# Order of the first loads, place of two groups of bulk loads, and a last stage that multiplies out of PSUM, in a kernel that mixes a long convolution with local attention

## The chip, the cores and the metric

The kernel runs on one core of a Trainium2 chip. The metric is the device time of one execution in microseconds. Before the change three runs took 224.1, 224.79 and 225.97 us; the median is 224.79. One execution of the same program was profiled; all rows below are of it, with times counted from its first instruction.

TensorE (PE in the rows; PEld is its weight load) multiplies matrices into PSUM, VectorE (DVE) and ScalarE (ACT) work element by element and empty PSUM, GpSimd (POOL) fills and copies in SBUF and issues DMAs, SyncE (SP) issues DMAs only. Each executes its own instructions in the order in which they are written and waits on semaphores where it needs another's result.

## The reference

Two branches over the same 2048 x 640 inputs are mixed by a gate (all bf16, batch of one):

```python
# A: causal long convolution of k_shift * v along the sequence, times q
k_shift = sum(k_pad[:, t:t + S] * shift_k[:, ks - 1 - t] for t in range(4))
kv = k_shift * v
y = causal_conv(kv, ssm_k) + kv * ssm_D          # in the reference by FFT of length 4096
a = q * y
# B: 32 heads of 20, each query sees 8 keys at distances 0, 2, ..., 14
qkv = x @ wqkv                                   # x is the same tensor as A's q
o = softmax(q . k_window / sqrt(20)) . v_window
b = o @ wo
# mix
g = sigmoid((x * gate_w).sum(-1))
out = g * a + (1 - g) * b
```

## The kernel before

The work is a set of generators ("streams"), each of which yields requests: `P` for TensorE, `A` or `D` or `AD` for ScalarE or VectorE, `G` for GpSimd, `S` for SyncE. `Steps.run` reads the string `ORDER` (L115): each letter names a stream and grants its next request, a `-` in front picks the second of two allowed engines. So `ORDER` fixes the instruction order of every engine by hand; the costs in the requests only document it. A stream that takes PSUM gets one of four double banks of the tile `PS`, first in, first out, and gives it back with the eviction.

The streams of the change, by their letter: `a` xpose, `c` fragger with the bulk loads inside it, `d` score_gen, `f` conv, `g` conv_v, `i` qkproj, `j` gate, `l` h_slot, `s` outproj, `t` final, `u` and `v` load_q(0) and load_q(1), `w` and `x` vproj(0) and vproj(1), `y` and `z` the forward transforms of the filter h.

The stages, in order of time:

- **Start** (`heads`, L396, and `xpose`, L439). x is loaded in eight pieces of 256 rows (`xn`, L413) on SP's queue, with the first half of the value weights (`Wv`, L407) after piece 0 and the first query and key weights (`Wqk`, L411) after piece 2. While the first loads run TensorE multiplies zeros (`WARM` = 7 matmuls of 512 columns, L401), and after the transposes of piece 0 four more of 512 columns with no use for the result (L447). `xpose` turns each piece by ten transposes into PSUM (L445) and one copy of 1280 columns into `xT` (even rows of x in its first half, odd ones in its second).
- **Projections and attention.** `vproj(0)` and `vproj(1)` make the values of 16 heads each, in 18 units of five matmuls (nine blocks, even and odd rows; L521), cast into `VW` (L524). Beside each head's 20 values `VW` holds a column of ones for the sum of the softmax; three memsets write it (L431 and L433). `qkproj` makes queries and keys in five tiles of 128 columns (`ft`, L568), cast to a staging tile `stg`; `fragger` copies each head's rows from there by DMA into `qb` and `kb` (L618, on GpSimd's queue but for the first tile), where `score_gen` reads them (L642), ScalarE takes exponentials (L650) and `pv_gen` multiplies with the values (L674).
- **Bulk loads** (`bulk`, L363) come behind the copies of a tile in `fragger`: k, small tables and the first half of h behind tile 0; G (the stage matrix of the second transform step, four loads of 384 KB) and the first half of v (four loads of 320 KB) in turn behind tile 1; the second half of v behind tile 2; the second half of h behind tile 3. `paced` (L326) has GpSimd write one element of the target first, and the load on SP waits for it, so that no load starts before GpSimd has come past the copies ahead of it.
- **Convolution.** `conv` makes the shifted k (L467 to L482), `conv_v` multiplies v by it (L486), two instructions on each half of v. The transforms (L701, L705, L724), products (L756) and `inverse1` (L835) follow; `h_slot` adds the direct term to h (L773) when a half of it has landed.
- **Last stage.** `inverse1(1)` ends with casts into `UC`. `outproj` makes b in 32 units of five matmuls (16 rows t, two halves n; L869), each evicted with the factor 1 - g into `bl` (L874 on ScalarE, L876 on VectorE). `load_q` loads q and multiplies it by g (L890). `final` (L893) works on six groups of rows t, `TAIL` = (0,3), (3,3), (6,2), (8,3), (11,3), (14,2): 32 small matmuls a row into two double banks (L912); two casts into `yb`, one by each engine (L919); on VectorE `q *= yb` (L924) and `q += bl` (L926); four output DMAs (L929). The g_nat loads of the gate (L543) stand on SP's queue ahead of the second half of h.

Of the kernel before, what the change touches and what calls it, by code (L numbers as in the profile page):

```python
# [18 lines left out]
D = 640  # L19
# [28 lines left out]
WARM = 7  # L48
KROWS = [(42, 64), (20, 42), (0, 20)]
TAIL = [(0, 3), (3, 3), (6, 2), (8, 3), (11, 3), (14, 2)]  # L50
# [65 lines left out]
a-aa-aw-wa-aw-ww-wiiai-iiaaiaa-aia-iii-aiaa-ii-iiii-ii-iiiicifffccccw-wwww-wwwwfwwwwf-wffffwwwwwwcwcccccwwwdw-wdwddddi-wfccccccii  # L116
-iiidfifddiiiieiifiiffiieidddiiiiiicddiwdxwexxxxxxxxxxccccffcfffffffffeccc-xcfcccccccccccccccccccccccccccccccccccccccccccidi-iiddd
ii-iddifd-iifxdddxedidffdfddefcicccii-iddiedd-icddlie-iiiyf-yddccdixiyyfy-xe-ydddexixdxddyyfyy-xcccxcccxffcccccccccccccciiiiciiccd
ciieddffdcccffdd-iiieiifiidididxdiffffffexididxdfeidid-i-xfxxyyy-yyexyey-xyyfyxccccccccciccccc-xcccc-idddidx-i-xxddddi-x-ijdddfjff
ejiddcciddcceiiiidddiiiiiffgg-ideieddd-ii-igigddiddeddjddeyjjyyyeeyyy-yyyy-yyyycc-yyyy-ycccccyyccccccccccccccclccccdddddz-zzd-zddd  # L120
z-zzzz-zzccczz-zzzzzz-zeddddedcdzdd-zedddoezdddd-zzo-zz-zjuddedddzedzz-zzzeezzz-zzooozz-z101-0010-1u111-111111-1o101-00o00-000000o
-00001011-1r-rr-r000u0r-r10111r00o00oooo2222-r0r-r000000000oqssss11110sssssss0s01111ssss2ss21111ssss222222222oooooooo222222244111p
313333p31333333333333413333uu4uuu444444444444444u54vv55u-5555-55-55-55-5555555tuut-ttssssssvvtvvstttstssssssv-tttvtttstssvv-ssvtvs
ttstst-ttssssssstttst-ttsssssssstttts-tssstt
# [91 lines left out]
def kernel(  # L216
# [146 lines left out]
    def bulk(ft):  # L363
        if ft == 0:
            yield from load_k(1)
            yield from load_k(2)
            yield from load_corners()
            yield from small()
            yield from load_h(0)
        if ft == 1:  # L370
            for a in range(4):
                yield from load_G(a)
                yield from load_v(0, a)
        if ft == 2:
# [21 lines left out]
    def heads():  # L396
# [8 lines left out]
        for a in range(8):  # L405
            if a == 1:
# [24 lines left out]
        nc.vector.memset(VW[:, :, :, DH], 1.0)  # L431
        for j in (0, NBP):
            nc.vector.memset(VW[0:PRE, j, :, DH], 0.0)  # L433
# [5 lines left out]
    def xpose():  # L439
        for a in range(8):  # L440
# [5 lines left out]
            for n in range(0 if a else 4):  # L446
                nc.tensor.matmul(PS[:, 3, 0], lhsT=ident[:], rhs=xn[:, 0, n % 2, 0:512], start=True, stop=True, skip_group_check=True)  # L447
# [411 lines left out]
    def outproj():  # L859
# [4 lines left out]
        for t in range(16):  # L864
            for n in range(2):
                g = yield Req("P", 0.0, [ev(f"oT{ft}") for ft in range(NDT)], take=1, half=1, pe=(5, 137.0, 272.0, 133.0))
                op = psum(g)[:, 0:320]
                for ft in range(NDT):
                    nc.tensor.matmul(op, lhsT=oT[:, ft].rearrange("p h m a -> p a (h m)")[:, t, :], rhs=wo[:, ft, 320 * n:320 * n + 320],  # L869
                                     start=(ft == 0), stop=(ft == NDT - 1), skip_group_check=True)  # L870
                r = yield Req("AD", dict(A=370.0, D=400.0), [g.done], give=g.banks)
# [5 lines left out]
            mark(f"bl{t}", r)  # L877
# [92 lines left out]
```

## Time and profile before

| | us |
|---|---|
| runs: lowest, median, highest | 224.1, 224.79, 225.97 |
| profiled execution, first to last instruction (its span) | 222.5 |
| of it busy: TensorE matmuls, VectorE, ScalarE, GpSimd | 204.3, 185.0, 174.9, 51.1 |
| first matmul on a piece of x | 4.57 |
| first query unit | 10.33 |
| last matmul of the second inverse step begins | 194.85 |
| first matmul of the last stage | 196.22 |
| last instruction of VectorE begins | 217.46 |

The profile gives no other time of the profiled execution than its span; the runs lie 1.6 to 3.5 us above that. A timeline row reads: start, length, engine, line, operation, output and inputs, count, and in brackets how long the engine had stood idle before and what ended that. Rows with a count are several instructions merged into one. SPq, ACTq and POOLq are the engines' own queues of issues.

### The profile page before, as it was taken

What the parts mean: (1) busy time and instruction counts of PE and PEld (TensorE: products, weight loads), DVE (VectorE), ACT (ScalarE), POOL (GpSimd) and SP (SyncE); (2) the same over time, 40 slices, a digit from 0 to 9 for tenths busy, and PEclk for the clock granted to TensorE, in tenths of its full rate; (3) what the DMA queues carried; (4) which work ended last, traced back from release to release, by engine and by line L of the source; (5) the groups of instructions that cost most, each with busy time, mean ns of one, the idle gap of its engine ahead of it and who ended that gap; (6) DMA issues with size and microseconds to landing.
All of it is one profiled execution on the core that took longest, in us unless ns stands there. A gap on an engine that the chain in (4) does not pass through costs nothing.

```text
span 222.5 us, 8401 instructions
## 1 busy us (share of the span) xinstructions
PE 204.3 (92%) x3577; PEld 165.8 (75%) x3577; DVE 185.0 (83%) x261; ACT 174.9 (79%) x253; POOL 51.1 (23%) x129
## 2 busy tenths in 40 slices
PE   7999999999999999699997867999999999979990
PEld 3777987696777577466685756889888899979880
DVE  4745778997998898569898978998999997859992
ACT  0264487769998898599999988998999999478770
POOL 7980711470617044402450000000000000000000
PEclk9999999999999999999999699999999999999999
DMA  6999789599999999803993396678567082003645
GB/s 199 349 237 275 188 180 205 133 168 149 208 182 197 163 151 155 140 4 52 183 171 74 85 214 152 172 174 213 122 142 227 4 184 55 3 3 91 152 106 136
DMA packets 69049, 33.35 MB, mean 150 GB/s; under 512 B 51476, under 2 KB 66708, under 8 KB 69012
## 3 DMA queue, kind: packets, MB, share of 16 engines
q1 hardware_dynamic: 65684, 27.66, 61.3%
q0 software_dynamic: 2880, 4.90, 9.9%
q8 instruction: 28, 0.46, 1.0%
q10 hardware_dynamic: 448, 0.26, 0.4%
q14 instruction: 9, 0.07, 0.1%
HBM read 19.51 MB, written 2.62 MB: 100 GB/s over the span
## 4 chain that ended last, share of the span: by engine, by line
PE 51%; DVE 20%; ACT 10%; DMA 8%; issue 7%; POOL 2%; DVEq 0%; POOLq 0%; ACTq 0%
PE PS L568 14%; PE PS L521 8%; ACT ETall L650 6%; PE PS L835 6%; DMA kb<-stg 6%; DVE UC L245 5%; PE PS L869 4%; PE PS L724 4%; PE PS L674 3%; DVE SX L245 3%; PE PS L642 3%; DVE q L926 2%; DVE yb L245 2%; ACT H L243 2%; DVE q L924 2%
## 5 line engine op out<-in xcount | busy, mean ns | idle before, releaser
L650 ACT ACTIVATE ETall<-PS 121x912 bf16<-121x912 f32 (+1 forms) x80 | 63.8, 864 | 8.1 <-PE PS L642 7.7
L568 PE MATMUL PS<-xT,Wqk 128*128 128x342 bf16 (+1 forms) x300 | 49.7, 310 | 0.6 <-ACT stg L243 0.3
L243 ACT CAST UC<-PS 128x1024 bf16<-128x1024 f32 (+2 forms) x49 | 44.4, 1030 | 4.0 <-DVE UC L245 3.1
L568 PEld LDWEIGHTS <-Wqk 128*128 128x128 bf16 x300 | 27.4, 97 | 14.3 <-issue 0.5
L521 PE MATMUL PS<-WvT,xT 128*121 128x320 bf16 x180 | 27.5, 300 | 0.1
L467 DVE TENSOR_TENSOR KX<-KX 128x1280 bf16<-128x1280 bf16 x32 | 25.3, 820 | 0.3
L618 POOL DMA_DIRECT2D qb<-stg x29 | 14.6, 506 | 45.8 <-ACT stg L243 30.5
L869 PE MATMUL PS<-wo,oT 128*128 128x320 bf16 x160 | 24.4, 302 | 0.1
L521 PEld LDWEIGHTS <-xT 128*121 128x121 bf16 x180 | 23.4, 134 | 1.4
L243 ACT CAST stg<-PS 128x363 bf16<-128x363 f32 (+1 forms) x39 | 17.1, 471 | 7.8 <-PE PS L568 7.5
L869 PEld LDWEIGHTS <-oT 128*128 128x128 bf16 x160 | 21.1, 145 | 1.5 <-issue 0.5
L724 PEld LDWEIGHTS <-G 64*128 64x128 bf16 x512 | 18.2, 93 | 4.9 <-issue 3.7
L618 POOL DMA_DIRECT2D kb<-stg x36 | 18.1, 511 | 15.8 <-ACT stg L243 7.6
L642 PE MATMUL PS<-qb,kb 31*128 31x114 bf16 x576 | 16.0, 212 | 5.1 <-DMA kb<-stg 2.3
L245 DVE CAST stg<-PS 128x342 bf16<-128x342 f32 (+1 forms) x21 | 11.0, 522 | 11.7 <-PE PS L568 9.4
L642 PEld LDWEIGHTS <-kb 31*128 31x128 bf16 x576 | 9.4, 93 | 13.5 <-issue 9.8
L674 PEld LDWEIGHTS <-ETall 121*128 121x128 bf16 x576 | 17.4, 96 | 2.1 <-issue 0.5
L674 PE MATMUL PS<-VW,ETall 121*128 121x63 bf16 (+2 forms) x576 | 18.2, 184 | 0.6 <-DVE SX L245 0.3
L835 PE MATMUL PS<-F,Hw 128*128 128x128 bf16 x160 | 18.1, 219 | 0.0
L874 ACT ACTIVATE bl<-PS,omg 128x320 bf16<-128x320 f32 x31 | 16.1, 566 | 2.4 <-PE PS L869 1.9
L835 PEld LDWEIGHTS <-Hw 128*128 128x128 bf16 x160 | 17.9, 114 | 0.0
L245 DVE CAST UC<-PS 128x1024 bf16<-128x1024 f32 x13 | 15.3, 1219 | 2.6 <-ACT UC L243 1.2
(75 smaller groups left out, 334.1 us busy)
## 6 DMA issues: line engine op xcount, KB each, us to landing
xn<-in_A_q_dram SPq DMA_DIRECT2D x8, 320.0 KB
h_lin<-in_A_ssm_k_dram SPq DMA_DIRECT2D x16, 160.0 KB
vin<-in_A_v_dram SPq DMA_DIRECT2D x8, 320.0 KB
Hw<-H SPq DMA_DIRECT2D x8, 320.0 KB
q<-in_A_q_dram SPq DMA_DIRECT2D x8, 320.0 KB
Hw<-SX SPq DMA_DIRECT2D x8, 320.0 KB
kb<-stg POOLq DMA_DIRECT2D x28, 85.1 KB, 5.5
out_dram<-q SPq DMA_DIRECT2D x16, 120.0 KB
```

The source lines that it names most:

```text
L243: nc.scalar.copy(dst, src)
L245: nc.vector.tensor_copy(dst, src)
L467: eng.tensor_tensor(d, kin[:, n + 3 - j:n + 3 - j + m, :], w.to_broadcast([128, m, QC]), ALU.mult)
L521: nc.tensor.matmul(ps[0:BK, 0:320], lhsT=xT[:, dt, s0:s0 + BK], rhs=Wv[:, dt, 320 * hp:320 * hp + 320], start=(dt == 0), stop=(dt == NDT - 1))
L568: nc.tensor.matmul(ps[:, 0:n], lhsT=Wqk[:, dt, w, 128 * ft:128 * ft + 128], rhs=xT[:, dt, s0:s0 + n], start=(dt == 0), stop=(dt == NDT - 1))
L618: (nc.sync if near else nc.gpsimd).dma_start(dst[r0:r0 + rows, 0:wd], stg[fa - f0:fb - f0, 0:wd])
L642: nc.tensor.matmul(psum(g, h4 // 2)[:, h4 % 2, BQ * bb:BQ * bb + BQ], lhsT=kb[r:r + DH + NF, BK * b:BK * b + 128], rhs=qb[r:r + DH + NF, B ...
L650: nc.scalar.activation(ETall[0:BK, e, :, 0:BQ * nb], psum(g, k)[0:BK, :, 0:BQ * nb], ACT.Exp, scale=SCALE)
L674: nc.tensor.matmul(O[:, (b - b0) // 6, c0:c0 + 21 * nh], lhsT=ETall[0:BK, e, hh, BQ * bb:BQ * bb + 128], rhs=VW[0:BK, b, 4 * t + h4:4 * t ...
L724: nc.tensor.matmul(ps[:, c, 160 * jj:160 * jj + 160], lhsT=G[rows, j0 + jj, 64 - 64 * rr:192 - 64 * rr], rhs=Am[rows, rr].rearrange("p o ( ...
L835: nc.tensor.matmul(d, lhsT=st[(key, P)][:, c, o + il // 4, :, il % 4], rhs=M[:, k, :], start=(k == 0), stop=(k == 1), skip_group_check=True)
L869: nc.tensor.matmul(op, lhsT=oT[:, ft].rearrange("p h m a -> p a (h m)")[:, t, :], rhs=wo[:, ft, 320 * n:320 * n + 320], start=(ft == 0), s ...
```

## The change

At the start: piece 1 of x is loaded second and the first half of the value weights third; `WARM` is 5; the four matmuls behind piece 0's transposes are gone; piece 0 is copied in two halves (even rows, odd rows), both on VectorE; the memsets of VW's ones stand behind the copy of piece 7. In the order the two value units of block 0 come ahead of piece 2's transposes; before, one came ahead of it and one behind:

```
before:  a -a a -a w -w a -a w -w w -w i i ...
after:   a -a -a a -a w -w w -w a -a w -w i i ...
```

The bulk loads: behind tile 1 only G; behind tile 2 the first half of v; behind tile 3 the second half of v and then the second half of h, as before. Everything else in the order of the middle stays.

The last stage. ScalarE casts the first half of a group into `yb` (now half as wide), VectorE multiplies the second half straight out of PSUM, then the first half from `yb`, and adds `bl` to both. Row 15 is left out of that addition: its two projection units come last, and VectorE adds them out of PSUM with the factor 1 - g in one instruction (`scalar_tensor_tensor`), followed by the outputs of that row. The order from the last cast of the inverse step on (O8.0 is row 8, half 0 of the projection, T0 to T5 the groups; each O is the matmuls and the eviction):

```
before:  q0 scale x2, T0 matmuls, cast, cast, O5.1 O6.0 O6.1, T0 mul, q1 scale x2, O7.0, T0 add,
         T1 ..., q1 scale x6 spread over T1 and T2, ... T5 matmuls, cast, O15.0, cast, O15.1, T5 mul, T5 add
after:   O5.1 O6.0, q0 scale x2, q1 scale x8,
         T0 (matmuls, cast, PSUM mul, mul, add), O6.1 O7.0 O7.1 O8.0,
         T1, O8.1 O9.0 O9.1, T2, O10.0 O10.1 O11.0, T3, O11.1 O12.0 O12.1,
         T4 matmuls, cast, PSUM mul, mul, O13.0 O13.1, T4 add,
         T5 matmuls, cast, PSUM mul, mul, O14.0 O14.1, T5 add (row 14), O15.0 O15.1
```

Two projection units thus stand ahead of T0, the ten scalings of q stand ahead of T0's arithmetic, and of the 31 evictions that ScalarE made of the projection and the one that VectorE made, 30 are now ScalarE's and two are the fused ones.

```diff
-WARM = 7
+WARM = 5
+LATE = 15
@@ bulk
             for a in range(4):
                 yield from load_G(a)
-                yield from load_v(0, a)
         if ft == 2:
             for a in range(4):
+                yield from load_v(0, a)
+        if ft == 3:
+            for a in range(4):
                 yield from load_v(1, a)
-        if ft == 3:
             yield from load_h(1)
@@ heads
-            if a == 1:
+            if a == 2:
                 nc.sync.dma_start(Wv[:, :, 0:320], W3[:, :, 2, 0:320])
...
-        nc.vector.memset(VW[:, :, :, DH], 1.0)
-        for j in (0, NBP):
-            nc.vector.memset(VW[0:PRE, j, :, DH], 0.0)
@@ xpose
-            for n in range(0 if a else 4):
-                nc.tensor.matmul(PS[:, 3, 0], lhsT=ident[:], rhs=xn[:, 0, n % 2, 0:512], start=True, stop=True, skip_group_check=True)
-            r = yield Req("AD", dict(A=1120.0, D=735.0), [g.done], give=g.banks)
...
+            for e in ((0, 1), (1, 2)) if a == 0 else ((0, 2),):
+                last = e[1] == 2
+                r = yield Req("AD", dict(A=1120.0, D=735.0) if a else dict(A=580.0, D=450.0), [g.done], give=g.banks if last else [])
...
             mark(f"xT{a}", r)
+            if a == 7:
+                nc.vector.memset(VW[:, :, :, DH], 1.0)
+                for j in (0, NBP):
+                    nc.vector.memset(VW[0:PRE, j, :, DH], 0.0)
@@ outproj
+                if t >= LATE:
+                    yield Req("D", 400.0, [g.done, ev(f"z{t}")], give=g.banks)
+                    reg = st["q1"][:, t % 8, 320 * n:320 * n + 320]
+                    nc.vector.scalar_tensor_tensor(reg, op, omg[:, t:t + 1], reg, ALU.mult, ALU.add)
+                    if n:
+                        for gg in range(4):
+                            (nc.scalar if gg > 1 else nc.sync).dma_start(...)
+                    continue
@@ final
-        yb2 = p0.tile([128, 2, 3, D], BF, name="yb2", tag="H0")
+        yb2 = p0.tile([128, 2, 3, 320], BF, name="yb2", tag="H0")
...
-            for k in range(2):
-                r = yield Req("AD", n=320 * m, deps=[g.done, ybfree[n % 2]], give=[g.banks[k]])
-                copy(r.eng, yb[:, 0:m, 320 * k:320 * k + 320].rearrange("p t (q c) -> p q t c", q=2),
-                     pss[k][:, :, 0:160 * m].rearrange("p q (t c) -> p q t c", c=160))
-                es.append(r.done)
...
-            nc.vector.tensor_tensor(reg, yb[:, 0:m, :], reg, ALU.mult)
...
+            r0 = yield Req("A", n=320 * m, deps=[g.done, ybfree[n % 2]], give=[g.banks[0]])
+            nc.scalar.copy(yb[:, 0:m].rearrange("p t (q c) -> p q t c", q=2), y[0])
+            yield Req("D", 75.0 + 1.04 * 320 * m, [g.done, ev(f"qg{t0 // 8}"), ev("qi1")], give=[g.banks[1]])
+            nc.vector.tensor_tensor(zq[1], y[1], zq[1], ALU.mult)
+            r = yield Req("D", 68.0 + 0.52 * 320 * m, [r0.done])
+            nc.vector.tensor_tensor(zs[0], yb[:, 0:m], zs[0], ALU.mult)
...
+            m = min(m, LATE - t0)
+            reg = reg[:, 0:m]
             r = yield Req("D", 100.0 + 0.52 * 640 * m, [ev(f"bl{t}") for t in range(t0, t0 + m)])
             nc.vector.tensor_tensor(reg, reg, st["bl"][:, t0:t0 + m, :], ALU.add)
...
-                (nc.scalar if n == len(TAIL) - 1 and gg > 1 else nc.sync).dma_start(...)
+                (nc.scalar if t0 + m == LATE and gg > 1 else nc.sync).dma_start(...)
```

More of the change, by code (lines that the diff above doesn't have):

```diff
@@ L115 @@
 ORDER = """
[L116 to L124, printed above, removed]
+a-a-aa-aw-ww-wa-aw-wiiai-iiaaiaa-aia-iii-aiaa-ii-iiii-ii-iiiicifffccccw-wwww-wwwwfwwwwf-wffffwwwwwwcwcccccwwwdw-wdwddddi-wfcccccci
+i-iiidfifddiiiieiifiiffiieidddiiiiiicddiwdxwexxxxxxxxxxccccffcfffffffffeccc-xcfcccccccccccccccccccccccccccccccccccccccccccidi-ii
+dddii-iddifd-iifxdddxedidffdfddefcicccii-iddiedd-icddlie-iiiyf-yddccdixiyyfy-xe-ydddexixdxddyyfyy-xcccxxffccccccccciiiiciiccdcii
+eddffdcccccccccccffdd-iiieiifiidididxdiffffffexididxdfeidid-i-xfxxyyy-yyexyey-xyyfyxciccccc-xcccc-idddidx-i-xxddddi-x-ijdddfjffe
+jiddcciddcccccccccceiiiidddiiiiiffgg-ideieddd-ii-igigddiddeddjddeyjjyyyeeyyy-yyyy-yyyycc-yyyy-ycccccyyccccccccccccccclccccdddddz
+-zzd-zdddz-zzzz-zzccczz-zzzzzz-zeddddedcdzdd-zedddoezdddd-zzo-zz-zjuddedddzedzz-zzzeezzz-zzooozz-z101-0010-1u111-111111-1o101-00
+o00-000000o-00001011-1r-rr-r000u0r-r10111r00o00oooo2222-r0r-r000000000oqssss11110sssssss0s01111ssss2ss21111ssss222222222oooooooo
+222222244111p313333p31333333333333413333uu4uuu444444444444444u54vv55u-5555-55-55-55-5555555ssssuuvvvvvvvvvvttttttsssssssstttttts
+sssssttttttssssssttttttsssssstttttssssttttttsssstssss
 """
@@ L876, in outproj @@
                     nc.vector.tensor_scalar(dst, op, omg[:, t:t + 1], None, ALU.mult)
-            mark(f"bl{t}", r)
+            if t < LATE:
+                mark(f"bl{t}", r)
         mark("outproj", g)
@@ L915, in final @@
             yb = yb2[:, n % 2]
-            es = []
-            for k in range(2):
-                r = yield Req("AD", n=320 * m, deps=[g.done, ybfree[n % 2]], give=[g.banks[k]])
-                copy(r.eng, yb[:, 0:m, 320 * k:320 * k + 320].rearrange("p t (q c) -> p q t c", q=2),
-                     pss[k][:, :, 0:160 * m].rearrange("p q (t c) -> p q t c", c=160))
-                es.append(r.done)
-            yield Req("D", 68.0 + 0.52 * 640 * m, es + [ev(f"qg{t0 // 8}"), ev("qi1")])
-            reg = st[f"q{t0 // 8}"][:, t0 % 8:t0 % 8 + m, :]
-            nc.vector.tensor_tensor(reg, yb[:, 0:m, :], reg, ALU.mult)
+            reg = st[f"q{t0 // 8}"][:, t0 % 8:t0 % 8 + m, :]
+            zs = [reg[:, :, 320 * k:320 * k + 320] for k in range(2)]
+            zq = [z.rearrange("p t (q c) -> p q t c", q=2) for z in zs]
+            y = [pss[k][:, :, 0:160 * m].rearrange("p q (t c) -> p q t c", c=160) for k in range(2)]
+            r0 = yield Req("A", n=320 * m, deps=[g.done, ybfree[n % 2]], give=[g.banks[0]])
[4 more added lines that the diff above has]
+            nc.vector.tensor_tensor(zs[0], yb[:, 0:m], zs[0], ALU.mult)
+            ybfree[n % 2] = r.done
+            for t in range(t0, t0 + m):
+                mark(f"z{t}", r)
+            m = min(m, LATE - t0)
+            reg = reg[:, 0:m]
             r = yield Req("D", 100.0 + 0.52 * 640 * m, [ev(f"bl{t}") for t in range(t0, t0 + m)])
             nc.vector.tensor_tensor(reg, reg, st["bl"][:, t0:t0 + m, :], ALU.add)
-            ybfree[n % 2] = r.done
             for gg in range(4):
-                (nc.scalar if n == len(TAIL) - 1 and gg > 1 else nc.sync).dma_start(raw(outf, (32 * (gg // 2) + gg % 2 + 2 * t0) * D, [[64 * D, 32], [2 * D, m], [1, D]]),
+                (nc.scalar if t0 + m == LATE and gg > 1 else nc.sync).dma_start(raw(outf, (32 * (gg // 2) + gg % 2 + 2 * t0) * D, [[64 * D, 32], [2 * D, m], [1, D]]),
                                   reg[32 * gg:32 * gg + 32])
```

8 lines of the change are left out of this document (5 added, 3 removed).

## The prediction

> **What bounds the kernel now.** I read the page first, then the timeline of the first 12 us, then the waits and the two-microsecond windows of the middle, then the timelines of TensorE, VectorE and ScalarE after 190 us.
>
> ```profile
> span 222.5 us, 8401 instructions
> PE 204.3 (92%) x3577; PEld 165.8 (75%) x3577; DVE 185.0 (83%) x261; ACT 174.9 (79%) x253; POOL 51.1 (23%) x129
> ```
>
> TensorE is busy 92% of the span and every engine runs its own instructions in a written order, so a change pays where it takes a hole out of TensorE's row (18 us of holes in all) or shortens what follows TensorE's last matmul. The change touches three places: the first 10 us, the loads between 55 and 104 us, and the last 28 us.
>
> The median of the runs (224.79) lies 2.3 us above this execution's span; I make the sum in the span and carry the difference to the median.
>
> **The start.** Timeline:
>
> ```profile
> 1.60 3.17 PE L401 MATMUL PS<-KX 128*128 128x512 bf16 x7 [1.60 <-DVE KX L398]
> ...
> 4.57 1.27 PE L445 MATMUL PS<-ident,xn 128*128 128x128 bf16 x10
> ...
> 5.63 1.63 PE L447 MATMUL PS<-xn,ident 128*128 128x512 bf16 x4
> 5.99 0.54 DVE L431 MEMSET VW<- 128x576 bf16 x1 [2.03 <-issue]
> ...
> 7.12 0.56 PEld L445 LDWEIGHTS <-xn 128*128 128x128 bf16 x10 [0.48 <-DMA xn<-in_A_q_dram]
> 7.12 0.73 PE L445 MATMUL PS<-ident,xn 128*128 128x128 bf16 x10
> ...
> 7.71 0.86 PE L521 MATMUL PS<-WvT,xT 128*121 128x320 bf16 x5
> ...
> 8.41 0.72 PE L445 MATMUL PS<-ident,xn 128*128 128x128 bf16 x10
> ...
> 8.97 1.52 PE L521 MATMUL PS<-WvT,xT 128*121 128x320 bf16 x10
> 9.17 0.82 DVE L245 COPY xT<-PS 128x1280 bf16<-128x1280 bf16 x1
> ...
> 10.33 0.89 PE L568 MATMUL PS<-xT,Wqk 128*128 128x342 bf16 x5
> ```
>
> The third load in the queue (piece 1 of x) lands at 7.12. Behind it TensorE is dense: transposes of piece 1, one value unit, transposes of piece 2, two value units, then the first query unit at 10.33.
>
> The change issues piece 1 second and the weights third. The bytes ahead of the third landing are the same, so I put the weights at 7.12. Piece 1 then lands between 4.14 and 7.12; by its 320 of the 720 KB about 5.5, and its ten transposes (1.07 us at the spacing of the L445 row at 4.57) end by 6.6. At 7.12 TensorE thus starts on the two value units of block 0, which need only piece 0: 2 x 0.69 = 1.4 us, to 8.5; transposes of piece 2 0.56, to 9.1; the value unit of block 1 0.69, to 9.8. The query unit needs the copy of piece 2 on VectorE: 9.1 + 0.1 + 0.82 = 10.0. Gain 0.35 to 0.55; I take **0.45**. The five warm-up matmuls for seven and the four dropped fillers free TensorE only while it waits for loads: nothing. The copy of piece 0 in two halves costs one more instruction on VectorE, under the wait for the weights: nothing; without that cover 0.1. The memsets of VW (0.54 and two short ones) go to about 17.7 us, where VectorE waits 0.5 to 1 us between casts of the query units: nothing; without cover 0.8. From 7.12 to 74 no load holds TensorE, so the 0.45 travels on.
>
> **The middle.** Timeline:
>
> ```profile
> 66.49 3.96 POOL L618 DMA_DIRECT2D kb<-stg  x8 [4.65 <-ACT stg L243]
> ...
> 74.99 0.38 PE L642 MATMUL PS<-qb,kb 31*128 31x114 bf16 x13 [0.38 <-DMA kb<-stg]
> ...
> 87.27 3.01 POOL L618 DMA_DIRECT2D kb<-stg  x6 [0.47 <-DVE stg L245]
> ...
> 93.46 0.38 PE L642 MATMUL PS<-qb,kb 31*128 31x114 bf16 x13 [1.92 <-DMA kb<-stg]
> ...
> 93.89 5.04 ACT L650 ACTIVATE ETall<-PS 121x912 bf16<-121x912 f32 x6 [2.31 <-PE PS L642]
> ...
> 104.22 2.89 DVE L486 TENSOR_TENSOR vin<-KX,vin 128x2560 bf16<-128x2560 bf16 x2
> ...
> 119.88 0.51 DVE L773 TENSOR_TENSOR h_lin<-h_lin,Dz 128x80 bf16<-128x80 bf16 x1
> ```
>
> The timeline of SP's queue alone:
>
> ```profile
> 70.08 16.73 SPq L323 DMA_DIRECT2D vin<-in_A_v_dram  x5
> 100.71 2.31 SPq L543 DMA_DIRECT2D g_nat<-WvT  x4
> 103.19 11.23 SPq L323 DMA_DIRECT2D h_lin<-in_A_ssm_k_dram  x8
> ```
>
> DMA issues (count, KB each, median us to landing):
>
> ```profile
> kb<-stg POOLq DMA_DIRECT2D x28, 85.1 KB, 5.5
> ...
> qb<-stg POOLq DMA_DIRECT2D x2, 64.1 KB, 3.9
> ```
>
> Windows (length; busy of PE, PEld, DVE, ACT, POOL; granted clock; DMA share; GB/s):
>
> ```profile
> 92.00:94.00 2.00, 0.54 (x15) 0.40 (x16) 0.10 (x1) 0.11 (x1) 0.00 (x0) 1.00 0.60 168
> ...
> 96.00:98.00 2.00, 2.00 (x31) 1.20 (x33) 1.04 (x3) 2.00 (x4) 0.00 (x0) 1.00 0.00 0
> ```
>
> Twice the scores wait for copies of keys out of the staging tile: 0.4 us before 74.99 and 1.92 before 93.46. In the second hole VectorE and ScalarE stand still too, so it costs the whole kernel its length. The copy issued at 87.27 is there at 93.46, 6.2 us later. It shares the DMA engines with the second half of v, whose five last loads hold SP from 70.08 to 86.8. The least crowded copies took 3.9, the median 5.5.
>
> The change leaves G alone at 55, sends the first half of v behind the third tile's copies (from 70.9, where the second half stood before) and the second half behind the fourth tile's, at about 90. At the pace of the SP row, 3.35 us a load, the first half is through by 71 + 13.4 = 84.4, ahead of the copy at 87.27. That one then takes 3.9 and lands at 91.2; TensorE arrived at 91.54 (93.46 less 1.92). The hole goes from 1.92 to between 0 and 0.45 (if the copy still takes 4.7, half way to the median). At 67 G alone is in flight in place of G and v, and the wait of 0.4 there needs only a copy quicker than 6.5: I count all of it. Sum **2.3**, less what comes late next.
>
> Late next is h_lin's second half. On SP the order is now second half of v, four small g_nat transfers, eight loads of h_lin; VectorE reads these at 119.88 (L773) and was busy up to there, so I cannot see slack, at most the 5.4 us after the last issue at 114.4. The second half of v has to pass between 90 and the h_lin issues, which now come at 103.19 - 2.75 = 100.4; the window at 96 shows the DMA engines empty. At 3.35 us a load it ends at 103.4, at the 168 GB/s of the window at 92 (1.28 MB, 7.6 us) at 98. Between, some 102: a stall of 0 to 2.7, and I charge 0.3. The multiplication by v (L486) needs the second half at 107 or later: covered. The middle gains **2.0**, between 0 and 2.4. If copies land late for another reason than v, nothing.
>
> **The end.** Timelines of TensorE and VectorE:
>
> ```profile
> 196.22 1.02 PE L912 MATMUL PS<-UC,SX 32*32 32x160 bf16 x96 [1.14 <-ACT UC L243]
> ...
> 197.17 2.94 PE L869 MATMUL PS<-wo,oT 128*128 128x320 bf16 x20
> ...
> 215.08 1.58 PE L869 MATMUL PS<-wo,oT 128*128 128x320 bf16 x10
> ...
> 197.26 1.16 DVE L245 CAST yb<-PS 128x960 bf16<-128x960 f32 x1 [2.23 <-PE PS L912]
> ...
> 217.46 0.83 DVE L926 TENSOR_TENSOR q<-q,bl 128x1280 bf16<-128x1280 bf16 x1
> ```
>
> Groups by form (count, busy, mean ns):
>
> ```profile
> L686 DVE TENSOR_TENSOR VW<-PS,rd 114x960 bf16<-114x960 f32 x8 | 9.3, 1158 | 0.3
> ...
> L756 DVE TENSOR_TENSOR Hw<-UC,Hw 128x960 bf16<-128x960 bf16 x20 | 13.1, 653 | 0.0
> ...
> L876 DVE TENSOR_SCALAR bl<-PS,omg 128x320 bf16<-128x320 f32 x1 | 0.5, 546 | 0.0
> ...
> L926 DVE TENSOR_TENSOR q<-q,bl 128x1920 bf16<-128x1920 bf16 x4 | 4.6, 1157 | 0.2
> ```
>
> And a window:
>
> ```profile
> 196.25:200.00 3.75, 3.75 (x116) 3.44 (x115) 2.63 (x4) 2.44 (x4) 0.00 (x0) 1.00 0.02 4
> ```
>
> TensorE rests 1.14 us up to 196.22, waiting for ScalarE's last cast of UC, and then has no hole to 216.66 (215.08 + 1.58). VectorE ends 1.63 later, at 218.29: its cast, multiplication and addition of the last group queue there. The output follows.
>
> Two of the 21 projection units left (0.72 us each, a fifth of 20 matmuls in 2.87 us) move into this rest. T0 then starts at 195.08 + 1.44 = 196.5, after its wait, and all that follows comes 1.14 earlier: TensorE ends at 215.5. VectorE no longer casts. A group of three has one multiplication from PSUM (1.16, by the L686 row, which also reads PSUM), one of half size in SBUF (0.6) and the addition (1.16), with gaps 3.0, where cast, multiplication and addition took 3.6. Its sum: four groups at 3.0, the short ones 2.2 and 1.8, two last instructions of 0.55: 17.1 us. Before T0 it scales q, ten instructions of 0.30 from 194.4 to 197.4; T0's matmuls end at 197.5, so this lies in VectorE's wait of 2.23. From 197.6 it would be done at 214.7, ahead of TensorE, which therefore sets the end. After the last projection comes one fused instruction from PSUM (0.55, L876's form) with one more queued ahead: 216.1 to 216.6 in place of 218.29. Two waits are new: the addition of group 4 waits for ScalarE's eviction of projection 13 with group 5's multiplication queued behind it, whose bank the last projection takes; and two outputs on ScalarE's queue wait for group 5's addition, with only the last two outputs behind them. ScalarE has 29 or fewer evictions of 0.56 and six casts, about 16 us of 20: covered. The outputs of the last row are half as large; four more issues of 0.4 on two queues go out as the data comes. The end gains 1.7 to 2.2, and I take **2.0**; below that 1.0, if VectorE's multiplications from PSUM hold up the next group's banks, above it 2.5.
>
> **Sum:** 0.45 + 2.0 + 2.0 = 4.45. Span 218.0, median **220.3**.
>
> **Rivals.**
>
> *The array's clock stays low at the start.* The L445 rows show the same ten transposes in 1.27 at 4.57 and 0.73 at 7.12: after 5.5 us of unbroken matmuls the rate doubled. The change breaks that run: between 3.7 and 7.12 TensorE would do two sets of transposes, 2.3 of 3.4 us. Against it:
>
> ```profile
> 120.00:122.00 2.00, 1.37 (x32) 0.88 (x32) 1.23 (x2) 2.00 (x4) 0.00 (x0) 1.00 0.28 65
> 122.00:124.00 2.00, 1.64 (x34) 1.24 (x35) 1.86 (x3) 2.00 (x4) 0.00 (x0) 0.73 0.98 234
> 124.00:126.00 2.00, 1.93 (x36) 1.67 (x32) 2.00 (x3) 2.00 (x3) 0.19 (x1) 0.50 0.15 37
> ```
>
> With TensorE 68% busy in one window the clock fell for some 3.4 us; at 92, 27% busy, it stayed at 1.00. So 68% may or may not do. At half rate the two value units end at 9.8 and the transposes of piece 2 at 10.5, the query unit starts at 11.5 instead of 10.0: 1.5 lost, 221.8. The Trainium skill, "TensorE: Matmul & The Clock Gate", Part 1, says that the clock is released only after a free-running window of about 3.4 us spent busy; by that rule the run up to 7.12 is what bought the full rate, and this trace agrees as far as the two L445 rows go.
>
> *The middle does not pay.* The copies are slow by themselves, or h_lin is late by what was won. Then 0.45 + 2.0, 222.3. For it: the least crowded copies still take 3.9.
>
> *Slower: the second half of v blocks SP.* Four loads now stand ahead of g_nat and h_lin. If they hold SP as long as the five did from 70.08, 16.7 us, they end at 107; g_nat's 2.3 follow, and h_lin is issued at 109, not 103.19. It lands 6 late, L773 stalls, and what was won before is swallowed. With 2.0 back at the end the time is 224.8 + 6 - 2 = 228.8. It decides from the point where the last v issue ends after 103 (100.71 and the 2.0 that the end gives back). Against it: that time SP stood behind G and the first half; at 90 the queue is nearly empty.
>
> **Chances.** Forecast 0.57 (its own range 219 to 221.3), low clock 0.15, middle without gain 0.20, blocked SP 0.08. A measurement here tells about 1%, 2.25 us, from nothing: faster means under 222.5. The forecast and the low clock lie there, and about a third of the middle's case: 0.77; within 1% 0.16; slower 0.07. The range 218.6 to 223.2 takes in the forecast, the clock and the middle's case.
>
> **What would show it.** Right: first query unit near 10.0; no DMA wait at the scores near 74 and 92; h_lin's addition at about 117; no TensorE hole at 195 less what was won; VectorE's last instruction within 1.2 us of TensorE's last. Wrong: value units at 0.27 us a matmul, L773 waiting on a DMA, or TensorE waiting for VectorE inside the last stage.

## The result and the profile after

The changed kernel took 232.5 us (median of four runs, 231.32 to 234.59) beside 224.94 for the kernel before (four runs, 224.1 to 225.97). The ratio is 1.032, 95% interval 1.0249 to 1.039: 3% slower, where 2% faster was forecast. Executions of one and the same kernel here differ by up to 3.6%; the medians below take in all of them, and the ratios leave out those more than 1.5% above the fastest.

The page of the changed kernel (its profiled execution took 231.32 us):

```profile
span 229.5 us, 8392 instructions
...
PE 205.8 (90%) x3571; PEld 167.6 (73%) x3571; DVE 183.4 (80%) x264; ACT 173.8 (76%) x251; POOL 50.8 (22%) x129
...
PEclk9799999999999999999967887999999999999997
```

TensorE did about as much work as before (204.3 us busy then) in a span that is 7.0 longer: holes were added. The row of the granted clock has a new dip in the second of its 40 slices (the start) and one in the 21st to 25th (115 to 143 us), where the kernel before shows one slice, the 23rd, below 9.

I matched the same instruction in both traces and took the difference of the starting times, stage by stage: +1.5 at the first query unit, +1.7 from 21 us on, +0.8 after the scores near 75, -1.3 after the scores near 93, +6.5 at the third multiplication by v, +8.0 at the end of the inverse step, +6.4 at VectorE's end, +7.0 at the end of the span. Four parts, then: the start lost 1.7, the two waits for keys gave 3.0, something near 110 cost 9.4, and the end gave 1.0. Of the 9.4, 7.8 are there when the third multiplication starts (-1.3 to +6.5); the other 1.6 come behind it and before 145 us, in the stretch where the clock dips.

**The loss near 110.** Timeline of SP's queue of the changed kernel:

```profile
72.29 6.37 SPq L324 DMA_DIRECT2D vin<-in_A_v_dram  x4
99.40 0.61 SPq L546 DMA_DIRECT2D g_nat<-WvT  x1
100.10 7.76 SPq L324 DMA_DIRECT2D vin<-in_A_v_dram  x4
107.92 5.25 SPq L546 DMA_DIRECT2D g_nat<-WvT  x3
113.33 10.13 SPq L324 DMA_DIRECT2D h_lin<-in_A_ssm_k_dram  x8
```

GpSimd released the second half of v early:

```profile
91.58 0.54 POOL L329 MEMSET vin<- 32x1 bf16 x4
```

But SP issues its four loads only from 100.10, and ahead of them stands one g_nat load. The waits of SP's queue from 64 to 125 us say what that load waited for (total, times, longest), first in the changed kernel and then in the kernel before:

```profile
SPq L546 <- ACT ETall L653: 21.3, 1, 21.3
```

```profile
SPq L543 <- ACT ETall L650: 14.5, 1, 14.5
```

Before, too, SP stood 14.5 us with a g_nat load at the head of its queue, which needs the row of the gate that ScalarE makes after exponentials near 100 us. It hurt nobody, as only h_lin was behind it. Now the second half of v is behind it. The other engines of the changed kernel, from their timelines:

```profile
112.34 0.80 PE L677 MATMUL PS<-VW,ETall 121*128 121x63 bf16 x24
116.48 2.90 DVE L489 TENSOR_TENSOR vin<-KX,vin 128x2560 bf16<-128x2560 bf16 x2 [7.70 <-DMA vin<-in_A_v_dram]
119.77 1.16 DVE L689 TENSOR_TENSOR VW<-PS,rd 114x960 bf16<-114x960 f32 x1
120.98 4.19 PE L727 MATMUL PS<-H,G 64*128 64x160 bf16 x76 [7.84 <-DVE VW L689]
122.01 0.96 ACT L244 CAST H<-PS 128x960 bf16<-128x960 f32 x1 [8.00 <-PE PS L727]
```

VectorE stands 7.70 us at the multiplication by v. Behind it in its order is the scaling of the attention's values (L689), which empties PSUM; TensorE has no bank until that is done and stands 7.84, and ScalarE waits 8.00 for TensorE. One load in the wrong place of one queue stopped three engines.

**The scores.** The wait of 1.92 before 93.46 is gone; the row that answers to it has no bracket:

```profile
92.10 0.39 PE L645 MATMUL PS<-qb,kb 31*128 31x114 bf16 x16
```

**The start**, timeline of TensorE:

```profile
3.85 0.99 PE L444 MATMUL PS<-ident,xn 128*128 128x128 bf16 x10
5.01 0.73 PE L444 MATMUL PS<-ident,xn 128*128 128x128 bf16 x10 [0.17 <-DMA xn<-in_A_q_dram]
7.40 2.43 PE L524 MATMUL PS<-WvT,xT 128*121 128x320 bf16 x10 [1.65 <-DMA WvT<-in_B_wqkv_dram]
9.62 1.27 PE L444 MATMUL PS<-ident,xn 128*128 128x128 bf16 x10
...
11.81 0.89 PE L571 MATMUL PS<-xT,Wqk 128*128 128x342 bf16 x5
```

The ten transposes take 0.73 at 5.01 and 1.27 again at 9.62: the rate had been high and fell after TensorE had stood 1.65 us waiting for the weights. In short windows the granted clock is 1.00 from 7.00 to 7.70, 0.73 from 7.70 to 8.00, 0.50 from 8.00 to 11.00 and 1.00 again from 11.30: it was halved from about 7.84 to 11.25, and the value units ran in that time. So the query unit came at 11.81, not at 10.0.

Another 0.2 went near 20 us. The row of the kernel before, then two of the changed kernel:

```profile
17.52 4.60 PE L568 MATMUL PS<-xT,Wqk 128*128 128x349 bf16 x30
```

```profile
19.00 4.82 PE L571 MATMUL PS<-xT,Wqk 128*128 128x349 bf16 x30
20.10 0.54 DVE L453 MEMSET VW<- 128x576 bf16 x1 [2.02 <-issue]
```

VectorE stands 2.02 us ahead of the moved memset of VW's ones, with the casts of the query units behind it, and TensorE's weight loads wait 0.4 for these casts.

**The end**, timelines of TensorE, VectorE and SP, and the last outputs that ScalarE issued in the kernel before:

```profile
204.41 1.02 PE L925 MATMUL PS<-UC,SX 32*32 32x160 bf16 x96
...
220.84 0.29 PE L925 MATMUL PS<-UC,SX 32*32 32x160 bf16 x17 [0.35 <-issue]
221.06 2.94 PE L872 MATMUL PS<-wo,oT 128*128 128x320 bf16 x20
...
223.65 1.00 DVE L877 SCALAR_TENSOR_TENSOR q<-PS,omg,q 128x320 bf16<-128x320 f32 x2
...
225.66 0.78 SPq L880 DMA_DIRECT2D out_dram<-q  x2
```

```profile
218.32 0.87 ACTq L929 DMA_DIRECT2D out_dram<-q  x2
```

VectorE ends 0.65 after TensorE, and no longer 1.63. But the last outputs are issued on SP 1.0 after their data was there (224.65), behind the outputs of the groups before; from VectorE's end to the end of the span 4.85 pass, where 4.21 did (218.29 to 222.5).

### The profile page after: what moved, and what is told of

Same layout as the page of the kernel before. It is cut to its first block, busy times and chain, and to the rows that moved or that the text cites. A ratio compares the mean times of both kernels' runs of the same rounds, so it can differ in the third digit from the quotient of the medians.

```text
span 229.5 us, 8392 instructions
## 1 busy us (share of the span) xinstructions
PE 205.8 (90%) x3571; PEld 167.6 (73%) x3571; DVE 183.4 (80%) x264; ACT 173.8 (76%) x251; POOL 50.8 (22%) x129
## 4 chain that ended last, share of the span: by engine, by line
PE 66%; DVE 13%; DMA 8%; ACT 5%; issue 4%; SPq 2%; DVEq 0%; ACTq 0%
PE PS L571 15%; PE PS L524 12%; PE PS L872 10%; PE PS L838 8%; PE PS L727 6%; DMA vin<-in_A_v_dram 5%; ACT ETall L653 4%; PE PS L677 4%; PE PS L645 3%; DVE SX L246 3%; DVE UC L246 3%; DMA WvT<-in_B_wqkv_dram 2%; PE PS L925 2%; PE PS L444 2%; SPq L324 2%
## 5 line engine op out<-in xcount | busy, mean ns | idle before, releaser
L524 PE MATMUL PS<-WvT,xT 128*121 128x320 bf16 x180 | 28.7, 309 | 1.8 <-DMA WvT<-in_B_wqkv_dram 1.6
L727 PEld LDWEIGHTS <-G 64*128 64x128 bf16 x512 | 20.3, 100 | 12.2 <-issue 11.1
L524 PEld LDWEIGHTS <-xT 128*121 128x121 bf16 x180 | 24.3, 138 | 3.3 <-issue 1.7
L621 POOL DMA_DIRECT2D qb<-stg x29 | 14.5, 504 | 43.3 <-ACT stg L244 27.2
L244 ACT CAST H<-PS 128x1024 bf16<-128x1024 f32 (+2 forms) x14 | 13.0, 977 | 9.1 <-PE PS L727 8.6
L246 DVE CAST SX<-PS 128x1024 bf16<-128x1024 f32 (+2 forms) x13 | 14.7, 1160 | 3.1 <-PE PS L727 2.1
```

Source lines behind the costliest of these rows:

```text
L244: nc.scalar.copy(dst, src)
L246: nc.vector.tensor_copy(dst, src)
L524: nc.tensor.matmul(ps[0:BK, 0:320], lhsT=xT[:, dt, s0:s0 + BK], rhs=Wv[:, dt, 320 * hp:320 * hp + 320], start=(dt == 0), stop=(dt == NDT - 1))
L621: (nc.sync if near else nc.gpsimd).dma_start(dst[r0:r0 + rows, 0:wd], stg[fa - f0:fb - f0, 0:wd])
L727: nc.tensor.matmul(ps[:, c, 160 * jj:160 * jj + 160], lhsT=G[rows, j0 + jj, 64 - 64 * rr:192 - 64 * rr], rhs=Am[rows, rr].rearrange("p o ( ...
```

## The experiments

Two theories for the loss near 110: **A**, it is the order on SP alone, a load that waits at the head of an in-order queue; **the rival**, the transfers themselves collide or v is too late at that place in any order, or part of the loss is the start's or the end's. For the start: the clock, or the changed order of the loads by itself.

### e1: the second half of v ahead of g_nat

In `ORDER` one letter of the stream `j` (gate) goes behind the letters `c` that issue v:

```diff
-...jiddcciddcccccccccceiiii...
+...iddcciddccccccccccjeiiii...
```

> The changed kernel with one token moved: the first g_nat load of the gate goes on SP's queue behind the four loads of v's second half, not ahead of them. Theory A (SP stood at g_nat's wait for ScalarE until 99.4 us with v queued behind it, and the multiplication by v waited 7.7 us): v's second half is issued at about 92, the wait of 7.7 before the third multiplication by v goes, TensorE's hole of 7.8 with it, and the clock's later dips with that; 232.5 - 9.4 = 223.1 us, with h_lin up to 1 us late 223 to 224.3. Rival B (v's second half is simply too much for the DMA engines between 90 and 110, whatever the order): a wait of 3 us or more stays, 226 us or more.

Measured: 223.11 us (221.78 to 226.39, ten runs) beside 225.36, ratio 0.9958 (0.9895 to 1.0021). SP and VectorE:

```profile
72.31 26.23 SPq L324 DMA_DIRECT2D vin<-in_A_v_dram  x8
99.41 3.40 SPq L546 DMA_DIRECT2D g_nat<-WvT  x4
102.98 13.99 SPq L324 DMA_DIRECT2D h_lin<-in_A_ssm_k_dram  x8
```

```profile
119.78 0.52 DVE L776 TENSOR_TENSOR h_lin<-h_lin,Dz 128x80 bf16<-128x80 bf16 x1 [1.11 <-DMA h_lin<-in_A_ssm_k_dram]
```

All of v is issued by 98.5, the early end of the prediction's 98 to 103.4, and no multiplication by v waits. One letter is worth 9.4 us on the median (232.5 to 223.11). What is late next is h_lin, by 1.11 here.

### e2: the start alone

The kernel before with the changed start only (`WARM = 5`, weights behind piece 1, the new order of the first units, the memsets later):

```diff
-WARM = 7
+WARM = 5
...
-            if a == 1:
+            if a == 2:
...
```

> The kernel before with the start of the changed one alone (piece 1 second, weights third, five warm-up matmuls, no fillers, values first, memsets of VW late). Theory A (the run of matmuls is broken by the wait for the weights and the array falls to half its rate for one period of 3.4 us): the first query unit at 11.8, TensorE 1.5 to 1.7 later from there on, 224.9 + 1.6 = 226.5 us. Rival B (the later landing of the weights, 7.35 for 7.07, is all there is): 225.0 to 225.3 us, and what the changed kernel lost at the start came from elsewhere.

Measured: 227.3 (222.53 to 228.98, ten runs) beside 225.36; ratio 0.9997 (0.99 to 1.0095). The profiled execution was the fastest of the ten, and shows the start as I had forecast it:

```profile
6.97 1.52 PE L523 MATMUL PS<-WvT,xT 128*121 128x320 bf16 x10 [1.04 <-DMA WvT<-in_B_wqkv_dram]
...
9.96 0.89 PE L570 MATMUL PS<-xT,Wqk 128*128 128x342 bf16 x5 [0.24 <-DVE xT L246]
```

The weights came at 6.93, the clock stayed up, the query unit came at 9.96, 0.37 ahead of the kernel before. The lead does not travel on: it is 0.15 after the memsets (24 us), and at the score unit at 32.06 both kernels are level. The span is 1.8 shorter all the same, as the waits for keys, to which nothing was done, were shorter in this execution. The median is 1.9 above that of the kernel before, but the ratio is 1.00, so e2 does not settle what the start costs in most executions.

### e3: the loads alone, v ahead of g_nat

The kernel before with the new places of the bulk loads and the letter of e1:

```diff
+        if ft == 2:
+            for a in range(4):
+                yield from load_v(0, a)
+        if ft == 3:
+            for a in range(4):
                 yield from load_v(1, a)
...
-...jiddcciddcceiiii...
+...iddcciddccccccccccjeiiii...
```

> The kernel before with the loads of v at the new places alone, and with g_nat's first load behind v's second half on SP. Theory A (the two waits of the scores for copies of keys came from v's loads, and only the order on SP spoiled the gain): the waits before 75 and 93 go, 0.9 and 2.1 us, and no new one comes: 224.9 - 3.0 = 221.9 us. Rival B (h_lin's second half, loaded behind v's, is late by what was won): 223.5 to 225 us with VectorE waiting for it at its addition to h_lin near 117.

Measured: 222.54 (221.25 to 224.8, ten runs) beside 225.36, ratio 0.9914 (0.9859 to 0.997). Against the kernel before the profiled execution is 0.8 ahead after the scores near 75, 2.9 after those near 93, and 2.95 to the end. TensorE, SP and VectorE:

```profile
90.53 0.38 PE L644 MATMUL PS<-qb,kb 31*128 31x114 bf16 x16
```

```profile
100.58 10.90 SPq L324 DMA_DIRECT2D h_lin<-in_A_ssm_k_dram  x8
```

```profile
117.00 0.52 DVE L775 TENSOR_TENSOR h_lin<-h_lin,Dz 128x80 bf16<-128x80 bf16 x1
```

Both waits for keys went and h_lin was in time, its issues at 100.58 where the prediction had put them at 100.4. This part of the change, with v ahead, is worth 2.8 on the median and 0.9% (1.9 us) by the ratio; I had given it 2.0, at most 2.4.

### e4: the last stage alone

The kernel before with the changed `outproj`, `final` and their order:

```diff
+                if t >= LATE:
+                    yield Req("D", 400.0, [g.done, ev(f"z{t}")], give=g.banks)
...
-            nc.vector.tensor_tensor(reg, yb[:, 0:m, :], reg, ALU.mult)
+            nc.vector.tensor_tensor(zq[1], y[1], zq[1], ALU.mult)
...
+            nc.vector.tensor_tensor(zs[0], yb[:, 0:m], zs[0], ALU.mult)
...
```

> The kernel before with the last stage of the changed one alone. Theory A (TensorE's hole before the last stage is filled and VectorE ends 1.7 earlier, but the outputs of the last groups leave SP's queue late, so that 4.8 in place of 4.2 us pass from VectorE's end to the end of the span): 224.9 - 1.0 = 223.9 us, VectorE's end at 216.6. Rival B (the prediction's term): the outputs leave as early as before behind VectorE's end, 222.9 us.

Measured: 223.8 (221.47 to 228.26, ten runs) beside 225.36, ratio 0.9979 (0.9916 to 1.0043). The span of the profiled execution, 219.7, is 2.8 below that of the kernel before. But 1.45 of it was there before the last stage, since the unchanged waits for keys were shorter in this execution; the stage itself gives 1.35. VectorE and SP:

```profile
213.91 1.00 DVE L875 SCALAR_TENSOR_TENSOR q<-PS,omg,q 128x320 bf16<-128x320 f32 x2
```

```profile
215.99 0.78 SPq L878 DMA_DIRECT2D out_dram<-q  x2
```

As in the changed kernel, SP issues the last outputs 1.1 after VectorE is done (214.91), and 4.8 pass from there to the end of the span, as A has it.

### e5: g_nat's first load on ScalarE's queue

The changed kernel with its own order; only the load at the head of SP's queue is issued by another engine:

```diff
-            nc.sync.dma_start(g_nat[32 * gg:32 * gg + 32, :], raw(src, ...))
+            (nc.sync if gg else nc.scalar).dma_start(g_nat[32 * gg:32 * gg + 32, :], raw(src, ...))
```

> The changed kernel with its own order, but the first of the four g_nat loads is issued by ScalarE's queue and not by SP's, so SP has nothing ahead of the second half of v that waits for the exponentials. Theory A (the 8 us are a wait at the head of SP's in-order queue): the second half of v is issued at 92, no wait at the multiplication by v, and the time is that of the version with v ahead, 223.1, plus 0.4 for ScalarE's issue: 223 to 224. Rival (the transfers themselves collide, or v at that place is late however it is issued): the multiplication by v still waits 3 us or more, 226 to 232.

Measured: 223.7 (221.93 to 226.09, ten runs) beside 224.92, ratio 0.9967 (0.9921 to 1.0012). SP, ScalarE and VectorE:

```profile
73.86 26.24 SPq L324 DMA_DIRECT2D vin<-in_A_v_dram  x8
```

```profile
101.08 1.13 ACTq L546 DMA_DIRECT2D g_nat<-WvT  x1
102.32 0.74 ACT L653 ACTIVATE ETall<-PS 121x684 bf16<-121x684 f32 x1 [1.26 <-PE PS L571]
```

```profile
111.43 2.88 DVE L489 TENSOR_TENSOR vin<-KX,vin 128x2560 bf16<-128x2560 bf16 x2
```

The order of the letters, the places and the bytes are those of the changed kernel, and the multiplication does not wait. It is the queue, as A says. The price of the issue on ScalarE was 1.1 (against the kernel before, the matched instructions around it go from +0.4 to +1.4), not 0.4: the next exponential starts late.

The Trainium skill ("DMA: Bandwidth & Descriptors", "Issuing engines are not separate DMA queues") says that issuing from several engines saves only the issuer's time, usually little. Here that saved 8.8 us on the median (232.5 to 223.7), since what it took away was not the issue itself (0.61 in the row at 99.40) but a wait that others stood behind; the measurement decides.

### e6: fillers at the start

e1 with six matmuls behind the transposes of piece 1:

```diff
+            for n in range(6 if a == 1 else 0):
+                nc.tensor.matmul(PS[:, 3, 0], lhsT=ident[:], rhs=xn[:, 0, n % 2, 0:512], start=True, stop=True, skip_group_check=True)
```

> The changed kernel with the second half of v ahead of g_nat, and six matmuls of 512 columns without use behind the transposes of piece 1, where TensorE waits for the value weights. Theory A (the 1.5 us at the start are the clock, which fell because TensorE stood still for 1.65 us before the weights came): the clock stays up, the query unit begins at 9.9 to 10.4 in place of 11.8, the time is 1.5 below the version without them, 221.6, and the runs lie closer together. Rival (the order of the loads itself costs the 1.5, by later landings): query unit at 11.5 or later, 223 to 224.

Measured: 222.1 (220.67 to 224.39, six runs) beside 224.92, ratio 0.9867 (0.9811 to 0.9924). TensorE:

```profile
5.97 1.46 PE L446 MATMUL PS<-xn,ident 128*128 128x512 bf16 x6
7.26 1.52 PE L526 MATMUL PS<-WvT,xT 128*121 128x320 bf16 x10
...
10.26 0.89 PE L573 MATMUL PS<-xT,Wqk 128*128 128x342 bf16 x5 [0.23 <-DVE xT L246]
```

TensorE is busy up to the value units, these run at the full rate (1.52 for ten, 2.43 in the changed kernel), and the query unit comes at 10.26. The profile alone does not decide, though: the weights, issued at 1.68 in both, landed at 6.69 here and at 7.35 in the changed kernel, and in e2 a landing at 6.93 kept the clock without fillers. What it shows is the price: the fillers held the value units by 0.6. The medians are on the side of A: 1.0 below e1 and e10 (223.11 and 223.09), not the 1.5 expected, and no query unit at 11.5. But by the ratio e6 (0.9867) and e10 (0.9878) are alike, so that the fillers pay is not shown.

### e7 and e11: the old start

e1 with the whole start of the kernel before, twice:

```diff
-WARM = 5
+WARM = 7
...
-            if a == 2:
+            if a == 1:
...
```

> The changed kernel with the second half of v ahead of g_nat, and the start of the kernel before (its loads' order, seven warm-up matmuls, four more behind piece 0's transposes, its order of units, the memsets of VW at the start). If the parts add: 225.4 - 2.8 (loads) - 1.6 (last stage) = 221.0, query unit at 10.3. Rival (the last stage and the loads share their gain, or the start is worth nothing on the median): 222.5 to 223.5, as the version with the changed start.

> The version with the start of the kernel before, v ahead and the changed last stage, once more: 222.3 as the first time, 1.0 to 2.0 below the one with the changed start if the start costs what the profile says, within 0.5 of it if not.

Measured: 222.28 (220.59 to 223.72, six runs) beside 224.92, ratio 0.9881 (0.9826 to 0.9936); and 222.63 (220.76 to 223.54, six runs) beside 225.27, ratio 0.9844 (0.9783 to 0.9906). Both medians are 2.64 below the kernel before, where the medians of the parts add to 4.4 (2.8 in e3, 1.6 in e4). By the ratios the parts add to 1.1% and the whole gives 1.2 and 1.6%. That the parts do not add is therefore not shown. The trace of e7 shows one place where a gain went in that execution. After the scores near 93 it is 2.92 ahead of the kernel before, after 140 only 0.92. Windows (length; busy of PE, PEld, DVE, ACT, POOL; granted clock; DMA share; GB/s):

```profile
120.00:124.00 4.00, 3.76 (x70) 3.09 (x63) 3.87 (x4) 3.61 (x5) 0.19 (x1) 0.50 0.35 91
...
132.00:136.00 4.00, 3.58 (x68) 2.76 (x64) 2.77 (x3) 3.29 (x5) 0.00 (x0) 0.50 0.64 145
```

The clock was halved in two spells here, from 119.6 to 126.5 and from 129.9 to 136.7 (by windows of 0.5 us), and in the kernel before in one of 3.4 us (0.73 and 0.50 in the windows that the prediction quotes). In e3 it was as before, and nothing was given back. One profile of each does not tell whether such spells belong to a kernel or to an execution: e1 and e10 are the same kernel, and in this stretch e1 has one spell of 6.8 us, e10 two.

### e8: the loads alone, in the changed order

The kernel before with the bulk loads at the new places and nothing else; the g_nat letter stays ahead of v:

```diff
+        if ft == 2:
+            for a in range(4):
+                yield from load_v(0, a)
+        if ft == 3:
+            for a in range(4):
                 yield from load_v(1, a)
...
```

> The kernel before with only the bulk loads at the changed places, in the changed kernel's own order, in which a g_nat load stands ahead of the second half of v. Theory A (the order on SP alone is the whole loss): the 2.8 gained by the loads and 9.4 lost at the multiplication by v: 232, a wait of 7 to 8 us for v on VectorE. Rival (part of the 9.4 is the slower clock of the start or the last stage, which only the whole change has): 227 to 229.

Measured: 232.93 (231.34 to 233.52, four runs) beside 224.92, ratio 1.0345 (1.0278 to 1.0412). SP and VectorE:

```profile
98.18 0.61 SPq L545 DMA_DIRECT2D g_nat<-WvT  x1
98.89 8.19 SPq L324 DMA_DIRECT2D vin<-in_A_v_dram  x4
```

```profile
115.12 2.89 DVE L488 TENSOR_TENSOR vin<-KX,vin 128x2560 bf16<-128x2560 bf16 x2 [7.56 <-DMA vin<-in_A_v_dram]
```

The moved loads alone make a loss as large as the whole change's: 232.93 beside its 232.5.

### e9: fillers where the clock falls

e7 with one matmul of 512 columns ahead of each of the 21 units of the transform of h's second half:

```diff
+        if key == "h" and P == 1:
+            nc.tensor.matmul(ps[:, 0, 0:512], lhsT=G[:, 0, 0:128], rhs=G[:, 0:4, 0:128], start=True, stop=True, skip_group_check=True)
...
```

> The version with the start of the kernel before, v ahead and the changed last stage, and in each of the 21 units of the transform of h's second half one matmul of 512 columns without use ahead of the unit's own, which overwrite it. Theory A (between 117 and 137 TensorE stands still so often that its clock falls, and this gave back 2.0 of the 2.9 that the loads had gained): the clock stays at 1.00 there, the middle keeps its 2.9, and the time is 1 to 2 below the version without them, 220.3 to 221.3. Rival (TensorE has no slack there and the fillers cost what they last, 21 x 0.22 = 4.6 at most): 223 to 227.

Measured: 226.92 (224.17 to 229.09, twelve runs) beside 225.27; ratio 1.0033 (0.9982 to 1.0084). The same two windows:

```profile
120.00:124.00 4.00, 3.90 (x47) 1.66 (x44) 2.93 (x3) 2.16 (x3) 0.19 (x1) 0.50 0.45 110
...
132.00:136.00 4.00, 3.00 (x78) 2.13 (x80) 2.32 (x4) 3.91 (x6) 0.00 (x0) 1.00 1.14 214
```

The second halving went and the first stayed; the stretch ahead of it holds only one filler, at 118.00. 4.3 us were lost on the median against e11, nearly the 4.6 of the rival, as if TensorE had no slack there. That the halved clock between 119 and 137 takes back part of the gain is thus seen in the profile of e7, but not shown by taking it away.

### e10: e1 once more, beside e11

The same kernel as e1, measured on the same chip as e11, for the price of the start by itself.

> The version with v ahead of g_nat and all else as changed, once more, on one chip with the next one, to price the changed start by itself. If the clock of the start costs 1.5 in most executions: 1.0 to 2.0 above the next one, 223.1 to 224. If not: within 0.5 of it.

Measured: 223.09 (221.15 to 224.38, six runs) beside 225.27, ratio 0.9878 (0.9812 to 0.9944): 0.46 above e11, within the 0.5 of the second case. In this profiled execution the weights came early and TensorE waited for nothing:

```profile
6.49 1.52 PE L524 MATMUL PS<-WvT,xT 128*121 128x320 bf16 x10
...
9.48 0.89 PE L571 MATMUL PS<-xT,Wqk 128*128 128x342 bf16 x5 [0.24 <-DVE xT L246]
```

Over the five profiled executions with the changed start and no fillers the order is always the same: the later the weights land, the later the query unit, and from some point the clock falls as well ("half": for about 3.4 us from 7.84, 8.16 and 9.30, after the value units had begun).

| | e10 | e2 | changed | e1 | e5 |
|---|---|---|---|---|---|
| weights landed | 6.44 | 6.93 | 7.35 | 7.53 | 8.56 |
| clock at the value units | full | full | half | half | half |
| query unit | 9.48 | 9.96 | 11.81 | 11.83 | 12.85 |

Over the seven with the old start the query unit is at 10.32 to 10.39 in every one. The changed start stakes 0.9 against up to 2.5, and the memsets take 0.2 of it in all six executions that move them: e10, 0.85 ahead at the query unit, is 0.62 ahead at 32 us. By the medians the start lost 0.5 here (e10 to e11) and 0.8 from e7 to e1 (measured apart), but the runs of each pair overlap, and e2 shows no difference by its ratio: that it does not gain is likely, what it costs stays open.

## Why the prediction was wrong

- **The step that failed** is the sentence "On SP the order is now second half of v, four small g_nat transfers, eight loads of h_lin". The first g_nat load stands ahead of the second half of v and waited for ScalarE until 99.40. From that sentence came "the multiplication by v (L486) needs the second half at 107 or later: covered"; the loads ended on SP at 107.86 and the multiplication waited to 116.48. With the order that I had written down, e1 and e3 show just what the sentence said: all of v issued by 98.5 and 96.5, no wait.
- **Why it failed.** I took the order of SP from the order of the loads in `fragger`, and the quiet of SP between 86.8 and 100.71 for an empty queue ("at 90 the queue is nearly empty"). It was a queue that waited: 14.5 us at the g_nat load, by the waits of SP in the trace of before, a view that I did not read for this stretch.
- **The rival of the blocked SP** had the right queue but not the size (4.0 lost on the whole, where 7.6 were; 6 at the stall, where 7.8 were) and the wrong culprit: v blocked by g_nat, not h_lin by v, and the stall at the multiplication by v, not at L773. Its 0.08 came from the misread queue.
- **The middle's gain**, sized at 2.0, is 3.0 against the execution that I had read: 0.9 and 2.1 in the changed kernel, 2.95 in e3. But in e2 and e4, where nothing was done to the loads, the same two places are 0.9 each ahead of that execution. Against those two the moved loads gave 1.2, all at the second place, so 1.8 of the 3.0 may be that execution's own. The five loads of the row at 70.08 are the last of the first half of v and the four of the second. "At 3.35 us a load" was too long where G is not in the queue: the row at 72.29 has four loads in 6.37, and in e1 v was through at 98.5, not near 102.
- **The start** went as its rival said in the changed kernel, e1 and e5 (query unit at 11.5 forecast, 11.81 measured), and as forecast or better in e2 and e10 (9.96 and 9.48). The step that failed is "I put the weights at 7.12" as one fixed time, where 6.44 to 8.56 were found, with the clock hanging on it. The Trainium skill ("TensorE: Matmul & The Clock Gate", Part 1) calls the window free-running, so that the same kernel finds it at another phase each time. This case agrees: with the old start the ten transposes that begin at 4.56 or 4.57 take 1.27 in five executions, 1.10 in e4 and 0.88 in e3. The same part gives at least one idle window of about 3.4 us as what throttles; here TensorE was busy for 1.59 of the 3.41 us ahead of the fall at 7.84, so that less was enough, and the measurement decides. My 0.15 leaned on the window at 92, 27% busy and yet at 1.00. TensorE stood 1.92 us there, longer than the 1.65 at the start, so the length of a stand alone does not decide, and that window could not rule the rival out.
- **The memsets of VW** "nothing; without cover 0.8", and "the 0.45 travels on": the term counted the 0.54 of the memset and not the 2.03 that VectorE stood ahead of it in the row at 5.99. The stand moved with it (2.02) and took 0.2 of the start in every execution that has it. The link is read from the waits; no run moved the memsets alone.
- **The end** was sized at 2.0 and gave 1.0 (1.35 in e4). VectorE was done 1.7 earlier against the last inverse step, at the low end of the 1.7 to 2.2 forecast: TensorE came 0.7 earlier and not 1.14, as it stood 0.35 inside the matmuls of T5. (A projection unit is a quarter of the 20 matmuls in 2.87, not a fifth; its 0.72 is right.) The step that failed is "four more issues of 0.4 on two queues go out as the data comes": SP issues its last outputs 1.0 after their data is there, where before the last two issues (ScalarE's, 218.32) followed VectorE's end at once. From VectorE's end to the end of the span 0.64 more pass than before, and with the 0.3 by which VectorE fell short of 2.0 that is the missing 1.0. That the late issues are what lengthens this stretch is argued from the rows; no run took them away.

With the order that I had assumed the kernel takes 223.1 (e1), within my range but 2.25 below the kernel before (225.36) where I had forecast 4.45. Of the 2.2 that are missing, the end has 1.0 and the start, by the medians, 1.0 to 1.3 (0.45 forecast as a gain, 0.5 to 0.8 lost). The middle's larger gain, h_lin's 1.1 and the halved clock also enter, and I cannot tell them apart; that the errors leave 223.1 inside the range is partly luck.

## What to carry to other kernels

Before a transfer is moved in a written order, list what the new queue holds ahead of it and what each of those waits for; an idle issuing queue may be an empty one or a waiting one, and only its waits tell which. A small load that depends on late arithmetic belongs behind every bulk load of its queue, or on another engine's queue. A gain at a first load is a stake on when it lands: look at the landing in several executions, and at the clock that a late one costs, before counting it.

## What the runs showed of the hardware that was not expected

- A load issued at the same 1.68 us landed between 6.44 and 8.56 in six executions, and the granted clock halves for about 3.4 us (7.84 to 11.25 in the changed kernel) or a multiple (6.8 from 117.1), at places that differ from execution to execution. The time of one kernel spreads from 222.3 to 230.31 (31 runs of the kernel before); how much of that is the clock and how much the loads is not shown.
- One DMA issued on ScalarE's queue between two exponentials cost the chain 1.1 us (e5), for an issue of 1.13.
- A memset of 0.54 us on VectorE has a stand of 2.02 or 2.03 us ahead of it that nothing in the profile explains, at either of its two places (5.99 before, 20.10 in the changed kernel).
- A filler matmul where TensorE shows holes of 0.2 to 0.8 us between short units is not free: 21 of them cost 4.3 us on the median (e9). Six in one hole ahead of a load did no harm (e6).
